# A gated state-space and linear-attention kernel: the convolution's kernel from two-factor tables by 32 channels, its parameters in polar form with n on the partitions, and FFT stages per 128 channels

## The chip, the cores and the metric

One core of one Trainium2 chip runs the kernel. The metric is the device time of one execution in microseconds (us), the median of the runs. Engines: PE is TensorE's matmul and PEld its weight load, DVE is VectorE, ACT is ScalarE, POOL is GpSimd, SP is SyncE, which here only issues DMAs.

## The reference

The input u has 2048 positions of 512 channels. Two branches are computed and mixed by a gate for each position:

```python
l = arange(L)                                        # L = 2048, D = 512, N = 128
P = exp(dt * A * l)                                  # complex, D x N x L
K = einsum("dn,dnl,dn->dl", Cc, P, dt * Bc).real
y = irfft(rfft(u padded to 2L) * rfft(K padded to 2L))[:L]
a = y + u * Dskip
pq, pk = q @ w_phi, k @ w_phi                        # 32 heads of 16
phi = concat(softmax(p), softmax(-p))
kv = sum_s phi_k v;  z = sum_s phi_k
b = ((phi_q @ kv) / (phi_q . z + 1e-6)) @ wo
g = sigmoid(sum(u * gate_w))
out = g * a + (1 - g) * b
```

## The kernel before

The program has four parts, one after the other. **Setup** loads u in two layouts (UD for the transform, xT for the attention), builds the transform's constants (TB, TI, TJ in `build_fft_consts`), turns A, B, C and dt into exponents and phases (`compute_params`) and writes these as pairs of bf16 rows through DRAM (pz) into four stationary tiles (statEL, statPL, statER, statPR). The spectrum of u, XU, is made here too (`u_path`). **Attention** (`part_b`) loads its weights, runs a loop over eight groups of 256 positions, multiplies all of Eq by the gate and denominator rows (aexp, L619 to L622), and then makes the output matmuls bps (L626, L628) into bS, which stays on chip.

**The convolution** goes over two halves of 256 channels (h). K of a channel is a product of a left factor (32 blocks of 64 positions) and a right factor (64 positions), summed over n on PE. Per 64 channels `exp_phase_q` makes E_L and E_R on ACT from argument matmuls. Per 32 channels `kgen_chunk` makes the phases: ACT computes k_y, k_anf, k_msinL, k_cosL, k_cosR, k_sinR; DVE multiplies them with E_L and E_R into k_Lre, k_mLim, k_Rre, k_Rim; PE makes 64 matmuls of 64 columns into kps (L234, L238); ACT casts to KD (L239), and `fft_stage_a` makes psA, evicted to XA. When all eight chunks are in XA, `k_slice_spectrum` runs over eight groups of two frequency rows: psB (L348), evicted to XK, two products t with XU on DVE (L380, L381), the inverse psz (L389), evicted to Z. Z is written to DRAM (Zd) and read back transposed (ZT) in two pieces, and `k_slice_out` makes psy, multiplies by the gate (ot) and writes the output. A scheduler orders each engine's instructions by its own estimates; buffers in the pools set what may run ahead.

Of the kernel before, what the change touches and what calls it, by code (L numbers as in the profile page):

```python
# [22 lines left out]

D = 512; N = 128; L = 2048


class KParams:
    pass


# [748 lines left out]
```

## Time and profile before

| | us |
|---|---|
| median of 3 runs (611.93 to 614.13) | 613.61 |
| profiled execution | 612.42 |
| its span | 609.9 |
| busy: ACT / PE / DVE / POOL | 309.9 / 304.6 / 285.4 / 51.6 |
| setup, until the attention's first matmul | 97.1 |
| attention | 140.0 |
| generator, spectrum, bounce and output, h = 0 | 115.4, 41.1, 28.2 |
| generator, spectrum, bounce and output, h = 1 | 113.8, 44.4, 29.9 |

No engine is busy for more than 51% of the span. The stages lie one after the other and have different limits, so the share of one engine over the span says little; each stage is to be read by itself, by what its last wait is for.

### The profile page before, as it was taken

The numbers are of one execution on the slowest core, as the hardware profiler recorded it, in microseconds if no ns is written. First come the engines' busy times: TensorE is split into PE (matmuls) and PEld (weight loads), VectorE is DVE, ScalarE is ACT, GpSimd is POOL, SyncE is SP. The second block draws the span as 40 slices with busy tenths as digits, with TensorE's granted clock in tenths as the row PEclk, the third lists the DMA queues.
The fourth block names the chain that finished last, engine by engine and source line by source line (L and its number), as shares of the span: only waits on it lengthen the run. The fifth ranks groups of instructions, "written<-read, shape, count | busy, mean of one in ns | idle before, by whom it ended". The sixth has DMA issues, their size and how long they took to land.

```text
span 609.9 us, 7578 instructions
## 1 busy us (share of the span) xinstructions
PE 304.6 (50%) x3168; PEld 150.0 (25%) x3168; DVE 285.4 (47%) x420; ACT 309.9 (51%) x384; POOL 51.6 (8%) x58
## 2 busy tenths in 40 slices
PE   0530346777858997252624346525252424356613
PEld 0430224433421353121212123301121212133300
DVE  6699953555567400626262645301626262635401
ACT  0541235799982125777768521106787768621202
POOL 7390570000000000000000000000000000000000
PEclk9975586899995799555557665655665768655555
DMA  9920280000000000000000003662000000001682
GB/s 256 234 43 1 70 205 6 0 1 0 2 2 0 1 0 1 0 1 1 0 2 0 2 1 97 103 82 66 0 1 1 0 2 0 2 1 72 68 138 69
DMA packets 44626, 23.31 MB, mean 38 GB/s; under 512 B 27952, under 2 KB 43312, under 8 KB 44080
## 3 DMA queue, kind: packets, MB, share of 16 engines
q1 hardware_dynamic: 21952, 12.59, 8.9%
q10 hardware_dynamic: 21488, 7.10, 7.2%
q0 software_dynamic: 1152, 3.15, 2.2%
q8 instruction: 24, 0.39, 0.3%
q14 instruction: 10, 0.08, 0.0%
HBM read 11.82 MB, written 9.96 MB: 36 GB/s over the span
## 4 chain that ended last, share of the span: by engine, by line
ACT 26%; PE 15%; DVE 6%; DMA 6%; issue 4%; ACTq 1%; SPq 0%
PE psz L389 5%; ACT E_R L189 4%; DMA ZT<-Zd 3%; PE psB L348 3%; PE psA L324 3%; ACT k_cosR L219 3%; ACT k_cosL L208 2%; ACT k_msinL L206 2%; ACT k_anf L204 2%; ACT k_sinR L220 2%; ACT E_L L181 2%; DVE t L380 2%; DVE XK L313 2%; ACT KD L239 2%; ACT L219 1%
## 5 line engine op out<-in xcount | busy, mean ns | idle before, releaser
L234 PE MATMUL kps<-k_Rre,k_Lre 128*32 128x64 bf16 x512 | 17.2, 241 | 102.9 <-DVE k_Lre L211 102.9
L190 DVE TENSOR_SCALAR nE_R<-E_R 128x2048 bf16<-128x2048 bf16 x8 | 5.6, 694 | 110.8 <-ACT E_R L189 110.8
L389 PE MATMUL psz<-t,TI 64*128 64x256 bf16 x256 | 30.6, 385 | 31.4 <-DVE t L380 31.4
L234 PEld LDWEIGHTS <-k_Lre 128*32 128x32 bf16 x512 | 13.7, 126 | 114.0 <-DVE k_Lre L211 114.0
L327 PE MATMUL psA<-W,UD 128*64 128x256 bf16 x128 | 13.9, 357 | 43.7 <-DMA UD<-in_A_u_dram 21.8
L626 PE MATMUL bps<-Mw,Eq 128*128 128x512 bf16 x128 | 31.8, 393 | 0.0
L189 ACT ACTIVATE E_R<-argps 128x1024 bf16<-128x1024 f32 x32 | 31.3, 1041 | 0.0
L630 ACT CAST bS<-bps 128x512 bf16<-128x512 f32 x16 | 9.4, 586 | 41.3 <-PE bps L628 41.3
L315 ACT CAST XK<-psB 128x1024 bf16<-128x1024 f32 x8 | 8.1, 1012 | 43.4 <-PE psB L348 43.4
L425 ACT ACTIVATE ot<-psy,gT 128x256 bf16<-128x256 f32 x16 | 6.7, 471 | 44.9 <-PE psy L416 35.4
L422 DVE TENSOR_TENSOR ot<-psy,gT 128x512 bf16<-128x512 f32 x8 | 5.5, 692 | 49.5 <-PE psy L416 38.6
L348 PEld LDWEIGHTS <-TB 64*64 64x64 bf16 x576 | 21.1, 146 | 30.4 <-issue 18.7
L186 PE MATMUL argps<-selR,statER 128*128 128x512 bf16 x64 | 25.4, 517 | 5.2 <-ACT E_R L189 2.9
L549 DVE TENSOR_TENSOR vr<-vp,vr 128x512 bf16<-128x512 f32 x32 | 19.9, 683 | 16.6 <-ACT vr L541 16.6
L239 ACT CAST KD<-kps 128x512 bf16<-128x512 f32 x16 | 9.4, 586 | 34.3 <-PE kps L238 34.3
L200 ACT ACTIVATE k_y<-argps 128x1024 f32<-128x1024 f32 x16 | 16.8, 1051 | 16.3 <-PE argps L197 16.3
L389 PEld LDWEIGHTS <-TI 64*128 64x128 bf16 x256 | 14.1, 121 | 41.5 <-DVE t L380 30.9
L537 DVE TENSOR_REDUCE Zk<-Ek 128x64 f32<-128x1024 bf16 x16 | 19.3, 1218 | 10.1 <-ACT Ek L536 9.5
L202 DVE SCALAR_TENSOR_TENSOR k_y<-k_y,argps 128x1024 f32<-128x1024 f32 x16 | 19.5, 1222 | 7.6 <-ACT k_y L200 7.6
L348 PE MATMUL psB<-XA,TB 64*64 64x128 bf16 (+1 forms) x384 | 21.1, 336 | 2.2 <-ACT XA L315 2.2
L324 PE MATMUL psA<-W,KD 128*128 128x256 bf16 x64 | 16.5, 414 | 11.0 <-ACT KD L239 11.0
L327 PEld LDWEIGHTS <-UD 128*64 128x64 bf16 x128 | 10.6, 202 | 45.3 <-issue 45.1
(222 smaller groups left out, 828.9 us busy)
## 6 DMA issues: line engine op xcount, KB each, us to landing
Zd<-Z SPq DMA_DIRECT2D x4, 1024.0 KB, 3.8
...
ZT<-Zd ACTq DMA_DIRECT2D x8, 256.0 KB, 8.0
ZT<-Zd SPq DMA_DIRECT2D x8, 256.0 KB, 7.6
out_dram<-ot SPq DMA_DIRECT2D x32, 32.0 KB, 1.6
out_dram<-ot ACTq DMA_DIRECT2D x32, 32.0 KB, 1.7
...
```

Source lines behind the costliest of these rows:

```text
L186: nc.tensor.matmul(ps[:, 8 * j:8 * j + 8, :], lhsT=kp.statER[:, G, :], rhs=kp.selR64[:, d0:d0 + 8, :], start=True, stop=True)
L189: nc.scalar.activation(out=E_R[:, dd:dd + 16, :], in_=ps[:], func=ACT.Exp)
L202: nc.vector.scalar_tensor_tensor(out=nf[:], in0=y[:], scalar=MAGIC, in1=ps[:], op0=ALU.subtract, op1=ALU.subtract)
L219: nc.scalar.activation(out=cosR[:], in_=ps2[:], func=ACT.Sin, scale=TWO_PI, bias=HALF_PI)
L234: nc.tensor.matmul(o, lhsT=Lre[:, dl, :], rhs=Rre[:, dl, :], start=True, stop=False, tile_position=(0, 32 * dj), skip_group_check=True)
L239: nc.scalar.copy(out=KD_dst, in_=kps[:].rearrange("p g e t -> p g (e t)"))
L324: nc.tensor.matmul(ps[:, i, :], lhsT=l[0], rhs=rhs, start=True, stop=True)
L327: nc.tensor.matmul(ps[64 * e:64 * e + 64, i, :], lhsT=l[e], rhs=rhs, start=True, stop=True, tile_position=(0, 64 * e))
L348: nc.tensor.matmul(o, lhsT=fc.TB[rows, r, op, :], rhs=rhs, start=(op == 0), stop=(op == 2), tile_position=(64 * e, 64 * rpar), skip_group_ ...
L389: nc.tensor.matmul(psz[:, rpar, sl, :], lhsT=fc.TI[rows, rh0 + sl, b0:b0 + 2, :].rearrange("p a b -> p (a b)"), rhs=rhs, start=(op == 0), ...
L549: nc.vector.tensor_tensor(out=vr[:, u, sg, :, 0:128].rearrange("p m (h e) -> p m h e", e=16), in0=vp[:].rearrange("p (m h e) -> p m h e", ...
L626: nc.tensor.matmul(ps[:], lhsT=Eq[:, i // 4, i % 4, 128 * j:128 * j + 128], rhs=Mw[:, i, :], start=(i == 0), stop=False, skip_group_check= ...
```

## The change

- **Tables in place of activations.** The left factor of K is no longer made by Exp and Sin for each channel block. Two tables with all 512 channels are made once, in setup: Ctab (4 factors for every 512 positions, with C, B and dt in it) and Dtab (8 factors for every 64 positions inside). `kgen_tables` multiplies them on DVE, complex, by broadcast: A has 4×8 = 32 columns per channel. Only the right factor comes from ACT: `kgen_exp` and `kgen_trig` for 128 channels at a time, in that order.
- **Parameters.** `polar_half` computes the tables from the raw parameters, which are loaded transposed (n on the partitions, channels along the row), in two halves of 256 channels. Only dt·A goes through pz into one tile, stat.
- **Weights' layout.** A has the channel as its innermost dimension, so kps's 32 weight columns are read 32 elements apart.
- **Four blocks of 128 channels** (Q) in place of two halves of 256. psB's matmuls have 128 and 64 columns where they had 256 and 128, psz's 128 where they had 256, with twice the number; eviction tiles keep their 1024 columns. KD, XA, XK and Z are all evicted on ACT, ot by DVE alone.
- **The bounce** is issued inside the loop over groups, when half of Z is there, and all of Zd, ZT and out stand in SP's queue. Rows of ZT and out are 256 bytes where they were 512. psy has a buffer of its own, so a block's output may run beside the next block's work.
- **Attention** alternates aexp and bps for each 512 positions, and bS goes through DRAM (bSd). Its weights are loaded early, in SP's queue; xp_d goes to ACT's queue and UD to POOL's, ahead of POOL's own work.

```diff
+    kp = Bag()
+    kp.stat = persist.tile([128, 16, 128], BF16, name="stat")
+    kp.C = persist.tile([128, 2, 4, 512], BF16, name="Ctab")
+    kp.D = persist.tile([128, 2, 8, 512], BF16, name="Dtab")
...
+def compute_polar(nc, tp, kp, raw):
+    for h in range(2):
+        polar_half(nc, kp, tp, {k: v[:, 256 * h:256 * h + 256] for k, v in raw.items()}, slice(256 * h, 256 * h + 256))
+    return kp
+def polar_half(nc, kp, tp, raw, ds):
+    nc.scalar.preload_act_table_set(LN_EXP)
...
+    EC = tp.tile([128, 4, W], BF16, name="EC", tag="e4", bufs=1)
+    nc.scalar.activation(out=EC[:], in_=big[:], func=ACT.Exp)
+    ED = tp.tile([128, 8, W], BF16, name="ED", tag="e8", bufs=1)
+    for b in range(8):
+        nc.scalar.activation(out=ED[:, b, :], in_=are[:], func=ACT.Exp, scale=64.0 * (b - 3.5))
...
+    sc = trig4(fill_c)
+    nc.vector.tensor_tensor(out=kp.C[:, 0, :, ds], in0=EC[:], in1=sc[:, 1], op=ALU.mult)
+    nc.vector.tensor_tensor(out=kp.C[:, 1, :, ds], in0=EC[:], in1=sc[:, 0], op=ALU.mult)
...
+def kgen_exp(nc, kp, selE, ps_pool, E, G0):
+    for gi in range(E.shape[1] // 32):
+        for b2 in range(2):
...
+            nc.scalar.activation(out=E[:, 32 * gi + 16 * b2:32 * gi + 16 * b2 + 16, :], in_=ps[:], func=ACT.Exp)
+def kgen_trig(nc, kp, selE, ps_pool, cs, G0):
+    for gi in range(cs.shape[2] // 32):
...
+        nc.scalar.activation(out=cs[:, 0, 32 * gi:32 * gi + 32, :], in_=ps[:], func=ACT.Sin, scale=TWO_PI, bias=HALF_PI)
+        nc.scalar.activation(out=cs[:, 1, 32 * gi:32 * gi + 32, :], in_=ps[:], func=ACT.Sin, scale=TWO_PI)
+def kgen_tables(nc, kp, wk, E, cs, dl, d0, n):
+    R = wk.tile([128, 2, n, 64], BF16, name="R", bufs=2)
+    Es = E[:, dl:dl + n, :]
+    c = cs[:, 0, dl:dl + n, :]; s = cs[:, 1, dl:dl + n, :]
+    ns = wk.tile([128, n, 32], BF16, name="ns", bufs=1)
+    nc.vector.tensor_scalar(out=ns[:], in0=s, scalar1=-1.0, scalar2=None, op0=ALU.mult)
+    nc.vector.tensor_tensor(out=R[:, 0, :, 32:64], in0=Es[:, :, 32:64], in1=c, op=ALU.mult)
+    nc.vector.tensor_tensor(out=R[:, 0, :, 0:32], in0=Es[:, :, 0:32], in1=c[:, :, ::-1], op=ALU.mult)
+    nc.vector.tensor_tensor(out=R[:, 1, :, 32:64], in0=Es[:, :, 32:64], in1=s, op=ALU.mult)
+    nc.vector.tensor_tensor(out=R[:, 1, :, 0:32], in0=Es[:, :, 0:32], in1=ns[:, :, ::-1], op=ALU.mult)
+    A = wk.tile([128, 2, 4, 8, n], BF16, name="A", bufs=2)
+    tmp = wk.tile([128, 4, 8, n], BF16, name="Atmp", bufs=1)
+    def Cb(i):
+        return kp.C[:, i, :, d0:d0 + n].unsqueeze(2).to_broadcast([128, 4, 8, n])
+    def Db(i):
+        return kp.D[:, i, :, d0:d0 + n].unsqueeze(1).to_broadcast([128, 4, 8, n])
+    for o, (i0, j0), (i1, j1), op in ((0, (0, 0), (1, 1), ALU.add), (1, (0, 1), (1, 0), ALU.subtract)):
+        nc.vector.tensor_tensor(out=A[:, o], in0=Cb(i0), in1=Db(j0), op=ALU.mult)
+        nc.vector.tensor_tensor(out=tmp[:], in0=Cb(i1), in1=Db(j1), op=ALU.mult)
+        nc.vector.tensor_tensor(out=A[:, o], in0=A[:, o], in1=tmp[:], op=op)
+    return A, R
+def kgen_chunk(nc, psK, A, R, dl, KD, ev):
+    kps = psK.tile([128, 4, 2, 64], F32, name="kps", tag="bk")
+    for e in range(2):
+        for g4 in range(4):
+            for ri in range(2):
+                for dj in range(4):
+                    d = dl + 16 * e + 4 * dj + g4
+                    nc.tensor.matmul(kps[32 * dj:32 * dj + 32, g4, e, :], lhsT=A[:, ri, :, :, d].rearrange("p a b -> p (a b)"),
+                                     rhs=R[:, ri, d, :], start=(ri == 0), stop=(ri == 1), tile_position=(0, 32 * dj), skip_group_check=True)
+    ev(KD, kps[:].rearrange("p g e t -> p g (e t)"))
...
+        step = 32 // ngr
+        if (2 * rh0 + 2 * ns) % step == 0:
+            r0 = 2 * rh0 + 2 * ns - step
+            rs = slice(r0, r0 + step)
+            nc.sync.dma_start(out=Zd[:, :, rs, :].rearrange("i t r d -> (i t) r d"), in_=Z[:, rs, :])
+            for th in range(2):
+                for ri in range(2):
+                    p0 = 64 * th + 32 * ri + r0
+                    eng = nc.sync if ri == 0 else nc.sync
+                    eng.dma_start(out=ZT[p0:p0 + step, :, :], in_=Zd[ri, 32 * th:32 * th + 32, rs, :].rearrange("t r d -> r t d"))
...
+    nj = min(512 // nd, 4)
+    for j0 in [x for jp in range(8 // nj) for x in (nj * jp, 8 + nj * jp)]:
+        th = j0 // 8
+        rows = slice(64 * th, 64 * th + 64)
+        ps = psY.tile([128, nj, nd], F32, name="psy", tag="py")
+        nc.tensor.matmul(ps[:], lhsT=ident[:], rhs=bsrc(j0, nj), start=True, stop=False, skip_group_check=True)
...
+        ot = opool.tile([128, nj, nd], BF16, name="ot")
+        nc.vector.tensor_tensor(out=ot[:], in0=ps[:], in1=gT[:, j0:j0 + nj].unsqueeze(2).to_broadcast([128, nj, nd]), op=ALU.mult)
+        ov = out2d[:, d0:d0 + nd].rearrange("(q j c) d -> c q j d", q=32, j=16, c=4)
+        for c in range(4):
+            nc.sync.dma_start(out=ov[c, :, j0:j0 + nj, :], in_=ot[32 * c:32 * c + 32, :, :])
...
-            nc.sync.dma_start(out=xp_d[512 * J:512 * J + 512, :].rearrange("(jc q) d -> jc q d", q=32), in_=xv[16 * J:16 * J + 16])
+            nc.scalar.dma_start(out=xp_d[512 * J:512 * J + 512, :].rearrange("(jc q) d -> jc q d", q=32), in_=xv[16 * J:16 * J + 16])
...
+        raw = {}
+        for k, src in (("Cre", A_C_re), ("Bre", A_B_re), ("Cim", A_C_im), ("Bim", A_B_im), ("Are", A_A_re), ("Aim", A_A_im)):
+            raw[k] = rawp.tile([128, 512], BF16, name=k)
+            nc.sync.dma_start_transpose(out=raw[k][:].unsqueeze(1), in_=src)
+        raw["ld"] = rawp.tile([128, 512], BF16, name="ld")
+        nc.gpsimd.dma_start(out=raw["ld"][:], in_=A_log_dt.partition_broadcast(128))
+        UD = rawp.tile([128, 64, 128], BF16, name="UD")
+        for dj in range(4):
+            nc.gpsimd.dma_start(out=UD[32 * dj:32 * dj + 32, :, :], in_=x2d[:, 128 * dj:128 * dj + 128].rearrange("(q t) d -> q t d", t=64))
...
+            def sink(j, ps):
+                bs = wp.tile([128, 512], BF16, name="bs", bufs=2)
+                nc.scalar.copy(out=bs[:], in_=ps[:])
+                nc.sync.dma_start(out=bSd[j], in_=bs[:])
+            attention(nc, tc, (wp, kpool, kwk, psB, psC), xT, wts, sink, gT, icol, ident, ck.close)
...
-        nd = 256
-        for h in range(2):
-            d0 = nd * h
+        nd = 128
+        n = 32
+        kev = Evict(nc, "a")
+        for Q in range(4):
+            d0 = 128 * Q
             XA = fpool.tile([128, 32, 2, nd // 2], BF16, name="XA")
...
+            E = epool.tile([128, 128, 64], BF16, name="E")
+            cs = epool.tile([128, 2, 128, 32], BF16, name="cs")
+            kgen_exp(nc, kp, selE, psP, E, 4 * Q)
+            kgen_trig(nc, kp, selE, psP, cs, 4 * Q)
+            for ch in range(4):
+                A, R = kgen_tables(nc, kp, wk, E, cs, 32 * ch, d0 + 32 * ch, n)
+                KD = wk.tile([128, 4, 128], BF16, name="KD", bufs=2)
+                kgen_chunk(nc, psK, A, R, 0, KD[:], kev)
+                fft_stage_a(nc, fc, psP, [[KD[:, i, :]] for i in range(4)],
+                            XA[:].rearrange("p r i (c d g) -> p (r i) c d g", d=4, g=4)[:, :, ch, :, :], kev)
             Z = fpool.tile([128, 32, nd], BF16, name="Z")
             ZT = fpool.tile([128, 32, nd], BF16, name="ZT")
-            Zd = dram.tile([2, 64, 32, nd], BF16, name=f"Zd{h}")
-            k_slice_spectrum(nc, fc, XA, nd, tpool, XU, d0, Z, Zd, ZT, psP, ev, evz)
-            k_slice_out(nc, fc, ident, ZT, nd, d0, bS, gT, out2d, opool, psP)
+            bS = fpool.tile([128, 16, nd], BF16, name="bS")
+            nc.sync.dma_start(out=bS[:], in_=bSd[:, :, d0:d0 + nd].rearrange("j p d -> p j d"))
+            Zd = dram.tile([2, 64, 32, nd], BF16, name=f"Zd{Q}")
+            k_spectrum_inverse(nc, fc, XA, nd, tpool, XU, d0, Z, Zd, ZT, psP, kev, kev, 2)
+            k_out(nc, fc, ident, ZT, nd, d0, lambda j0, nj: bS[:, j0:j0 + nj, :], gT, out2d, opool, psK)
```

ACT's order, the generator of 64 channels in the kernel before (E_L, E_R are exponentials, argps the arguments in PSUM, k_ tiles the phases of 32 channels):

```order
L181 ACTIVATE E_L<-argps 128x1024
L189 ACTIVATE E_R<-argps 128x1024 x2
L181 ACTIVATE E_L<-argps 128x1024
L189 ACTIVATE E_R<-argps 128x1024 x2
L200 ACTIVATE k_y<-argps 128x1024
L219 ACT_TABLE_LOAD
L219 ACTIVATE k_cosR<-argps 128x1024
L204 ACTIVATE k_anf<-k_y 128x1024
L206 ACTIVATE k_msinL<-k_y 128x1024
L208 ACTIVATE k_cosL<-k_anf 128x1024
L220 ACTIVATE k_sinR<-argps 128x1024
L239 CAST KD<-kps 128x512
```

In the changed kernel, the start of the generator for 128 channels; Z is the last eviction of the block before, E and cs are the tables of the right factor:

```order
L277 ACT_TABLE_LOAD
L277 ACTIVATE E<-args 128x1024
L70 CAST Z<-psz 128x2x4x128
L277 ACTIVATE E<-args 128x1024 x7
L286 ACT_TABLE_LOAD
L286 ACTIVATE cs<-args 128x1024
L287 ACTIVATE cs<-args 128x1024
```

All of the block's exponentials now stand together, and the phases of the left factor are gone.

DVE's order in the changed kernel, from the end of the first block's tables to its first product t12 (A_2439 belongs to that block's last 32 channels, finished just before; A_3049 and A_3137 to the first two chunks of the next block):

```order
L311 TENSOR_TENSOR Atmp_3050<-Ctab_288,Dtab_289 128x1024
L312 TENSOR_TENSOR A_3049<-A_3049,Atmp_3050 128x1024
L311 TENSOR_TENSOR Atmp_3050<-Ctab_288,Dtab_289 128x1024
L310 TENSOR_TENSOR A_3137<-Ctab_288,Dtab_289 128x1024
L312 TENSOR_TENSOR A_3049<-A_3049,Atmp_3050 128x1024
L310 TENSOR_TENSOR A_3137<-Ctab_288,Dtab_289 128x1024
L311 TENSOR_TENSOR Atmp_3138<-Ctab_288,Dtab_289 128x1024
L312 TENSOR_TENSOR A_3137<-A_3137,Atmp_3138 128x1024
L311 TENSOR_TENSOR Atmp_3138<-Ctab_288,Dtab_289 128x1024
L312 TENSOR_TENSOR A_3137<-A_3137,Atmp_3138 128x1024
L386 TENSOR_TENSOR t12_2576<-XU_60,XK_2574 128x1024
L387 TENSOR_TENSOR t34_2577<-XU_60,XK_2574 128x1024
```

The next block's left tables are made before the spectrum of this block is multiplied.

SP's order in the changed kernel, around the end of block 2 and block 3 (Zd_4272 is block 2's, Zd_5146 block 3's):

```order
L402 DMA Zd_4272<-Z 128x2048 x2
L407 DMA ZT<-Zd_4272 16x32x128 x8
L426 DMA out_dram<-ot 32x4x128 x4
L402 DMA Zd_5146<-Z 128x2048
L426 DMA out_dram<-ot 32x4x128 x12
L727 DMA bS<-bSd 128x16x128
L407 DMA ZT<-Zd_5146 16x32x128 x4
L402 DMA Zd_5146<-Z 128x2048
L407 DMA ZT<-Zd_5146 16x32x128 x4
L426 DMA out_dram<-ot 32x4x128 x16
```

The last 12 outputs of block 2 stand between the first half of block 3's Z and the reads of ZT.

## Rows read from the trace of the kernel before

**Rows 1.** Stage table: us, busy time and count of each engine, granted clock, DMA share.
```profile
0.00:97.10 97.10, 26.95 (x385) 19.36 (x386) 75.25 (x126) 27.13 (x28) 51.55 (x58) 0.76 0.57 128
97.10:237.10 140.00, 118.19 (x736) 55.77 (x737) 67.27 (x112) 87.30 (x141) 0.00 (x0) 0.89 0.00 1
237.10:352.50 115.40, 47.88 (x624) 21.04 (x624) 48.51 (x64) 84.64 (x91) 0.00 (x0) 0.60 0.00 1
352.50:393.60 41.10, 24.00 (x324) 13.95 (x325) 20.14 (x24) 9.10 (x9) 0.00 (x0) 0.62 0.30 52
393.60:421.80 28.20, 9.57 (x82) 2.89 (x82) 2.77 (x4) 5.43 (x10) 0.00 (x0) 0.50 0.56 108
421.80:535.60 113.80, 44.06 (x618) 19.94 (x618) 48.51 (x64) 83.83 (x90) 0.00 (x0) 0.66 0.01 2
535.60:580.00 44.40, 27.26 (x324) 14.95 (x325) 20.14 (x24) 9.11 (x9) 0.00 (x0) 0.50 0.28 48
580.00:609.90 29.90, 6.69 (x76) 2.05 (x75) 2.77 (x4) 3.36 (x8) 0.00 (x0) 0.50 0.54 106
```

**Rows 2.** Timeline of ACT, first generator; start, duration, line, operation.
```profile
238.75 1.93 ACT L189 ACTIVATE E_R<-argps 128x1024 bf16<-128x1024 f32 x2
...
244.37 1.28 ACT L219 ACT_TABLE_LOAD   x1
```

**Rows 3.** Timeline of all engines, end of one chunk's chain.
```profile
319.69 0.69 DVE L211 TENSOR_TENSOR k_Lre<-E_L,k_cosL 128x1024 bf16<-128x1024 bf16 x1 [0.25 <-ACT k_cosL L208]
320.43 0.11 PEld L234 LDWEIGHTS <-k_Lre 128*32 128x32 bf16 x4 [6.61 <-DVE k_Lre L211]
320.44 0.25 PE L234 MATMUL kps<-k_Rre,k_Lre 128*32 128x64 bf16 x4 [5.71 <-DVE k_Lre L211]
...
323.25 1.01 ACT L315 CAST XA<-psA 128x1024 bf16<-128x1024 f32 x1 [1.13 <-PE psA L324]
```

**Rows 4.** Timeline of ACT, second spectrum, first and last row.
```profile
535.63 1.01 ACT L315 CAST XA<-psA 128x1024 bf16<-128x1024 f32 x1 [1.13 <-PE psA L324]
...
578.96 1.01 ACT L315 CAST Z<-psz 128x1024 bf16<-128x1024 f32 x1 [3.15 <-PE psz L389]
```

**Rows 5.** Groups of PE, second spectrum: busy us, mean ns, idle before.
```profile
L389 PE MATMUL psz<-t,TI 64*128 64x256 bf16 x128 | 16.5, 410 | 15.7 <-DVE t L380 15.7
L348 PE MATMUL psB<-XA,TB 64*64 64x128 bf16 (+1 forms) x192 | 11.0, 346 | 1.1 <-ACT XA L315 1.1
```

**Rows 6.** Groups of DVE, first generator.
```profile
L202 DVE SCALAR_TENSOR_TENSOR k_y<-k_y,argps 128x1024 f32<-128x1024 f32 x8 | 9.8, 1222 | 3.8 <-ACT k_y L200 3.8
...
L225 DVE TENSOR_TENSOR k_Rre<-E_R,k_cosR 128x1024 bf16<-128x1024 bf16 x8 | 5.5, 684 | 0.0
```

**Rows 7.** Costliest groups of the page: weight loads from strided columns.
```profile
L327 PEld LDWEIGHTS <-UD 128*64 128x64 bf16 x128 | 10.6, 202 | 45.3 <-issue 45.1
```

**Rows 8.** DMA issues of the page: KB each, us to landing.
```profile
Zd<-Z SPq DMA_DIRECT2D x4, 1024.0 KB, 3.8
...
ZT<-Zd SPq DMA_DIRECT2D x8, 256.0 KB, 7.6
out_dram<-ot SPq DMA_DIRECT2D x32, 32.0 KB, 1.6
```

**Rows 9.** Timeline of DVE, the last output.
```profile
603.24 0.69 DVE L422 TENSOR_TENSOR ot<-psy,gT 128x512 bf16<-128x512 f32 x1 [1.66 <-DMA out_dram<-ot]
```

**Rows 10.** Timelines of ACT's queue, DVE and PE in setup.
```profile
0.80 13.45 ACTq L683 DMA_DIRECT2D UD<-in_A_u_dram  x4
...
32.05 2.19 DVE L290 TENSOR_SCALAR TI<-TI 128x2048 bf16<-128x2048 bf16 x1
...
97.10 1.12 PE L496 MATMUL wps<-Wphi,wkT 128*128 128x128 bf16 x9 [13.32 <-DMA Wphi<-in_B_w_phi_dram]
```

**Rows 11.** Timeline of PE, first output matmuls of the attention.
```profile
203.58 3.41 PE L626 MATMUL bps<-Mw,Eq 128*128 128x512 bf16 x8
...
207.05 1.89 PE L626 MATMUL bps<-Mw,Eq 128*128 128x512 bf16 x8
```

More of the change, by code (lines that the diff above doesn't have):

```diff
@@ new lines, in kgen_exp @@
+def kgen_exp(nc, kp, selE, ps_pool, E, G0):
+    for gi in range(E.shape[1] // 32):
+        for b2 in range(2):
+            ps = ps_pool.tile([128, 16, 64], F32, name="args", tag="pb")
+            for j in range(2):
+                d0 = 16 * b2 + 8 * j
+                nc.tensor.matmul(ps[:, 8 * j:8 * j + 8, :], lhsT=kp.stat[0:64, G0 + gi, :], rhs=selE[0:64, d0:d0 + 8, :],
+                                 start=True, stop=True, tile_position=(0, 0))
+            nc.scalar.activation(out=E[:, 32 * gi + 16 * b2:32 * gi + 16 * b2 + 16, :], in_=ps[:], func=ACT.Exp)
@@ L409, in k_slice_out, with k_out @@
+def k_out(nc, fc, ident, ZT, nd, d0, bsrc, gT, out2d, opool, psY):
+    nj = min(512 // nd, 4)
[4 more added lines that the diff above has]
+        nc.tensor.matmul(ps[:], lhsT=ident[:], rhs=bsrc(j0, nj), start=True, stop=False, skip_group_check=True)
         for jj in range(nj):
[L410 to L412 removed]
@@ L596, in part_b @@
-        for sg in range(2):
-            nc.vector.tensor_tensor(out=den[:, sg, :], in0=Sps[sg][:], in1=rZ[:, sg, :], op=ALU.mult)
-        nc.vector.tensor_tensor(out=den[:, 0, :], in0=den[:, 0, :], in1=den[:, 1, :], op=ALU.add)
-        nc.scalar.activation(out=den[:, 0, :], in_=den[:, 0, :], func=ACT.Ln, bias=eps[:])
-        nc.vector.tensor_tensor(out=lnZ[:], in0=lnZ[:], in1=den[:, 0:1, :].to_broadcast([128, 2, 512]), op=ALU.add)
-        nc.scalar.activation(out=apm[:], in_=lnZ[:], func=ACT.Exp, scale=-1.0)
@@ L615, in part_b @@
-        for b in range(4):
-            for m in range(4):
-                for sg in range(2):
-                    ps = bank("aexp")
-                    nc.tensor.matmul(ps[:], lhsT=Xsel[32 * b:32 * b + 32, m, :], rhs=apm[32 * b:32 * b + 32, sg, :], start=True, stop=True,
-                                     tile_position=(32 * b, 0))
-                    e = Eq[:, sg, m, 512 * b:512 * b + 512]
-                    nc.vector.tensor_tensor(out=e, in0=e, in1=ps[:], op=ALU.mult)
-        for j in range(16):
+                ps = bank("aexp")
@@ L624, in part_b @@
+                nc.tensor.matmul(ps[:], lhsT=Xsel[32 * b:32 * b + 32, m, :], rhs=apm[32 * b:32 * b + 32, sg, :], start=True, stop=True,
+                                 tile_position=(32 * b, 0))
+                e = Eq[:, sg, m, 512 * b:512 * b + 512]
+                nc.vector.tensor_tensor(out=e, in0=e, in1=ps[:], op=ALU.mult)
+        for j in range(4 * b, 4 * b + 4):
             ps = bank("bps")
```

811 lines of the change are left out of this document (341 added, 470 removed).

## The prediction

> **What bounds the kernel now.** I read the stage table first [rows 1]. The profiled execution spans 609.9 us and took 612.42, so 2.5 us lie outside the span; it stands 1.2 us under the median of 613.61. Six of the eight stages do the convolution: twice a generator (115.4 and 113.8), a spectrum (41.1 and 44.4) and a bounce through DRAM with the output (28.2 and 29.9), 372.8 us together. In the generator ACT is busy 84.64 of 115.4 us, DVE 48.51, PE 47.88. In the bounce no engine works: PE 9.57 of 28.2, DMA 0.56. The generator's limit is a chain. ACT makes tables of 128x1024, two E_R in 1.93 us at 238.75, so 0.92 or so apiece, with 1.28 for a table load [rows 2]; per 128 channels it makes 36 (4 E_L, 8 E_R, and per 32 channels k_y, anf, msinL, cosL, cosR, sinR), with 4 table loads. Then ACT waits while the last table goes DVE → PE → ACT → PE → ACT [rows 3]: k_Lre runs from 319.69 to 320.38, kps starts at 320.44, XA at 323.25 and ends at 324.26, so 3.9 us pass from the table's end to XA's.
>
> The spectrum follows a generator and runs from XA's end at 536.64 to the last Z's end at 579.97, 43.3 us for 256 channels, at a granted clock of 0.50 (the 1.2 GHz level) [rows 1, 4]. PE waits there for t: psB x192 and psz x128 are 11.0 and 16.5 us busy of 43.3 [rows 5], and the rest is PE → eviction → t → PE → eviction with little overlap.
>
> **The generator.** ACT now makes per 128 channels 8 Exp (L277) and 8 Sin (L286/L287), with 2 table loads, in place of 36 and 4; ACT's rows in the second order fence show it. That is 20×0.92 + 2×1.28 [rows 2] = 21 us less of ACT per 128 channels. What comes in its place is DVE work: per 32 channels 6 two-input operations on the broadcast tables C and D (A, Atmp), 4 for R and a negation. For R and A the row is k_Rre L225, bf16 128x1024 at 684 ns [rows 6], which starts every 0.61 when back to back. L225 reads one input with step −1 at this price; no row reads bf16 inputs with step 0. So A's price lies between 0.61 and the 1.22 of the f32 operation of the same size [rows 6]; I take 0.61, since A's operands and result are bf16 as L225's are, and keep 1.22 for the range.
>
> By the Trainium skill, "VectorE: DVE Perf Modes", section "What auto-detection actually checks", a two-input operation takes its doubled mode where every tensor is 16-bit with step ±1; a step of 0 in an outer dimension is left open by that sentence. Row L225 agrees for step −1. If the mode were lost, the sum would be the one with 1.22 below; if not, mine.
>
> Each block of 128 channels is then a chain, and DVE's order (third fence) says where it can hide. The tables A of the next block's first two chunks stand ahead of the first t of the spectrum, so they cost nothing as long as DVE waits there for XA and XK; if that cover fails, 12×0.61 = 7 us come back per block. From the last Z: ACT has one E ahead of that Z, then 7×0.92 + 1.28 + 1.05 = 8.8 us to the first cosine. DVE then has 28 operations (16 R, 12 A of the last two chunks) × 0.61 and 4 negations of some 0.4 (half of 0.69): 18.7. The last chunk's kps → XA is 3.9 as now [rows 3]; its 64 matmuls take 0.9 us now, from 320.44 on, with four loads at a time. Its weights are now read with a stride of 32 elements; the nearest row is UD's, strided too, 202 ns a load [rows 7]. Four at a time, 64 such loads would take 3.2 us: the far bound is +2.3 per block. I take zero, since the loads overlap. The spectrum for 128 channels is half of 43.3: 21.7, since the number of evictions, t and columns halves. That is 53.1. Four psy/ot of the block before, set between XK and Z, add 1.5 (4 ot of 0.69 less what falls into waits), and I add 1.4 for more and narrower matmuls: **56 per block**, 224 for four, against 314.7 for the two generators and spectra [rows 1].
>
> The narrower matmuls are the main doubt. For the same 1024 columns per group psB now takes 48 matmuls instead of 24, and psz 32 instead of 16: over the kernel 1280 where 640 were. A matmul of 64 columns can follow the one before at 14 ns (64 kps in 0.9 us), so columns set the pace, not counts: about zero. The other bound keeps all of today's spectrum time in PE's count: 27.5 us over 320 matmuls [rows 5] is 86 ns for each, so 640 more are +55.
>
> **The bounce.** Block Q's Zd, ZT, psy and out now lie beside block Q+1's generator; for three of four blocks nothing waits for them. Before, 28.2 us in the middle were bare; I put that at 0. The cover is 35 us of generator against 3.8 (Zd) + 7.6 (ZT) and the outputs [rows 8]. At the end stays one bounce. Per block it is half as large, but SP's order (fourth fence) puts 12 outputs of block 2 between the two halves of Zd and all of ZT, and PE has eight psy behind the last psz. An ot waits for its buffer until earlier outputs have landed, as now at 603.24 (1.66 us, [rows 9]), so I count 2 us for each group of four outputs, of which landing is 1.6. That makes 4×2 for block 2's outputs, Zd and ZT 3.8 + 7.6, four psy/ot 4×2.1, and from the last ot's start to the end 6.7 as now (603.24 to 609.9): 34.5, some 35 instead of 29.9, **+5**.
>
> The Trainium skill, "DMA: Bandwidth & Descriptors", section "Specifications", speaks against this part: under 512 bytes a transfer leaves line rate, with a read-modify-write, and ZT and out now go in rows of 256 bytes. No row here tells 256 from 512 for ZT; if ZT took as long as today for half the bytes, 7.6 us, the sum above has it so already.
>
> **Setup.** Before, the first wps starts at 97.10, after 13.32 us of waiting for Wphi's loads [rows 10]; these now stand early in SP's queue, so the wait goes. But POOL now issues UD ahead of its own iotas: ACT needed 13.45 us for these four issues [rows 10], and DVE's constants (TI ends at 34.24 now) start some 10 us later: 45. Then the tables C and D: two halves of 256 columns, each a chain that goes back and forth between DVE (some 45 operations, 16 us by the rates of [rows 6] scaled to their columns) and ACT (12 us and 7 table loads of 1.28, 9 us), 37 alone, about 65 for both with one's ACT beside the other's DVE. With the last XU that puts wps at 111: **+14**, bounds −12 (all of the constants' delay hidden and the halves overlapped better) and +12.
>
> **Attention.** From 97.1 to 237.1 it takes 140.0 [rows 1]. Its loop is unchanged, two table loads per round included. The products Eq and the output matmuls alternate per 512 rows now, so each of the four output runs starts behind a stretch at half clock: the first eight bps matmuls of a run take 3.41 against 1.89 [rows 11], 3 times 1.5 more, with aexp's first latency and shorter evictions: **+6** (0 to +16). The first front, which has nothing beside it, adds 1.6.
>
> **Sum.** 609.9 + 14 + 6 + 1.6 − (314.7 − 224) − 28.2 + 5 = 517.6, with 2.5 outside **520 us**.
>
> **Rivals.** (a) A at the slow rate: 12 operations of the last two chunks per block × 0.61 is +7 to +8 per block, 552. For: no row with step 0; against: everything is bf16. (b) The spectrum is bound by the count of matmuls: +55, 575. For: PE is the longest link there; against: kps's 14 ns. (c) The bounce is not hidden, since SP's one queue holds Zd, ZT and out in an order in which each waits for the one before, and psy, in the middle of PE's order, holds back psz: up to 10 per block in three blocks, 550. (d) Slower than before: every added matmul costs its full latency, because four row and column tiles no longer overlap when each has half the columns. At psB's mean of 336 ns [rows 5] 640 more are +215, 735; it decides from (613.6 − 520)/640 = 146 ns each. The kps chain is against it. (e) The setup's chain overlaps fully and the spectrum reaches full clock (4.2 for 5.2 us in each of 16 groups): −12 − 16, 492.
>
> **How the numbers follow.** The forecast's case (500 to 545) 0.66, (a) 0.10, (b) 0.08, (c) 0.07, (e) 0.04, (d) 0.03, 0.02 for no change, should several of (a) to (c) meet. The range of 494 to 560 leaves out (b), (d) and the lower edge of (e). Change by less than 0.5%, 3 us, is about what a measurement of this kernel can't tell: faster 0.94, same 0.01, slower 0.05.
>
> **What would show it.** In the new profile: ACT busy some 32 of 56 us in a block; A (L310 to L312) near 0.69 mean; psB and psz with about unchanged total busy time for twice the count; no stretch of 28 us without engines in the middle; the first wps near 111; the last Z some 35 us before the end. The prediction is wrong if A has 1.2 in its row, if the time from XA to the last Z in a block is well over 22, or if setup lasts beyond 123.

## The result and the profile after

The changed kernel takes 541.18 us, median of 4 runs (540.47 to 541.62), against 613.87 (611.93 to 615.76) for the kernel before in the same session: ratio 0.8815, 95% interval 0.8786 to 0.8844. The forecast was 520 in a range of 494 to 560, so the gain is 73 us where 94 were expected. The profiled execution took 540.47, its span 538.7.

The stage table of the changed kernel, to be laid beside [rows 1], has the same columns. The first three rows are the setup up to the attention's first matmul wps at 141.16, the next two the attention (its loop; aexp and bps), then four blocks and the end:

```profile
0.00:34.80 34.80, 0.00 (x0) 0.18 (x1) 3.70 (x20) 0.01 (x1) 8.34 (x17) 1.00 1.08 177
34.80:88.00 53.20, 20.86 (x192) 15.35 (x192) 34.59 (x55) 27.20 (x38) 11.38 (x6) 1.00 0.37 85
88.00:141.30 53.30, 17.17 (x194) 9.13 (x194) 38.90 (x79) 39.47 (x50) 1.80 (x5) 1.00 0.00 1
141.30:229.50 88.20, 65.67 (x507) 34.71 (x513) 50.82 (x81) 77.03 (x122) 0.00 (x0) 0.96 0.00 1
229.50:281.00 51.50, 47.89 (x220) 20.61 (x222) 20.08 (x33) 9.35 (x16) 0.00 (x0) 0.86 0.12 38
281.00:336.90 55.90, 33.41 (x622) 20.17 (x622) 38.89 (x65) 32.57 (x37) 0.00 (x0) 0.53 0.17 32
336.90:394.10 57.20, 36.34 (x684) 21.77 (x683) 33.71 (x56) 31.66 (x36) 0.00 (x0) 0.50 0.15 29
394.10:449.60 55.50, 34.10 (x635) 20.66 (x634) 31.82 (x53) 31.64 (x35) 0.00 (x0) 0.50 0.34 51
449.60:502.50 52.90, 34.18 (x679) 20.85 (x678) 25.45 (x43) 29.23 (x33) 0.00 (x0) 0.53 0.38 59
502.50:538.70 36.20, 8.06 (x119) 3.14 (x118) 5.10 (x8) 0.02 (x1) 0.00 (x0) 0.50 0.65 102
```

Against the forecast's sum:

| us | forecast | measured | off |
|---|---|---|---|
| setup | 111.1 | 141.3 | +30.2 |
| attention | 146.0 | 139.7 | −6.3 |
| four blocks, with the first front | 225.6 | 221.5 | −4.1 |
| the end | 34.9 | 36.2 | +1.3 |
| span | 517.6 | 538.7 | +21.1 |

The convolution came out near its sum; the miss lies in the setup. For 34.8 us hardly an engine works, and then PE, DVE and ACT are busy for 38, 73 and 67 of another 106.

**The setup.** Timelines of the changed kernel, several engines; start, duration, engine, line, and in brackets the idle time before it and what ended it:

```profile
0.80 33.97 ACTq L639 DMA_DIRECT2D xp_d<-in_A_u_dram  x4
...
2.19 4.20 POOL L648 DMA_DIRECT2D UD<-in_A_u_dram  x4
...
34.80 1.28 ACT L182 ACT_TABLE_LOAD   x1 [34.80 <-DMA gw<-in_gate_w_dram]
...
37.82 1.29 DVE L84 TENSOR_SCALAR tg_v<-colB,if_p 128x2048 int32<-128x2048 f32 x1 [27.99 <-ACT w L87]
...
52.98 1.45 DVE L115 TENSOR_SCALAR TI<-TI 128x2048 bf16<-128x2048 bf16 x1
```

POOL needed 4.20 us for the four UD issues, not 13.45 as ACT in [rows 10]; its delay, which the forecast counted, is not there. ACT stands instead: the four xp_d issues hold its queue from 0.80 to 34.77, so it makes its first table entry at 37.38, DVE waits 27.99 us for it, and TI is done at 54.4, where it was done at 34.2 before [rows 10]. The row of 33.97 us is mostly waiting. All operations on xp_d (ns, shortest, median and longest; first and last start), and the profile's chain around the fourth issue (start, duration):

```profile
L639 ACTq DMA_DIRECT2D xp_d<-in_A_u_dram x4: 570/584/696, 0.8 to 34.2; - x4
```

```profile
29.92 4.25 DMA gw<-in_gate_w_dram
...
34.20 0.57 ACTq L639
```

An issue takes 0.57 to 0.70 us; the rest lies between them. The second starts at 25.08, when SP's transposed load Are has landed (issued at 6.16, landing 18.9 us later), the third at 27.18, with the landing of wkT (19.09, 8.1 later), the fourth behind the landing of gw. In the trace's records these three issues wait for the completion semaphores of Are, wkT and gw. So ACT waits for SP's loads, though it needs none of the three tiles yet. No run changes the semaphores alone.

The second loss is in the matmuls of u's spectrum. Groups of PE from 34 to 142 us in the changed kernel (busy, mean ns, idle before them and what ended it):

```profile
L338 PE MATMUL psA<-W,UD 128*64 128x256 bf16 x128 | 18.4, 422 | 56.6 <-DVE W L100 39.9 <-DVE XAu L68 9.6 <-ACT XAu L70 7.1
L359 PE MATMUL psB<-XAu,TB 64*64 64x256 bf16 (+1 forms) x192 | 17.1, 484 | 42.8 <-DVE XU L68 19.2 <-ACT XU L70 16.9 <-ACT XAu L70 6.7
```

psB waits 19.2 and 16.9 us for evictions XU. The full diff has a change that I hadn't shown or costed: `psA` and `psB` lost `bufs=3`. In the convolution they take the three buffers of their pool, but `u_path` runs in a pool of one (`ps0`), so each group of matmuls waits for the eviction of the one before, and each eviction stands in line between the polar operations on ACT and DVE.

**A block.** Groups from 281 to 502.5 us, to be laid beside [rows 5, 6]:

```profile
L395 PE MATMUL psz<-t,TI 64*128 64x128 bf16 x512 | 35.4, 305 | 30.7 <-DVE t L386 30.5 <-DVE t L387 0.2
...
L312 DVE TENSOR_TENSOR A<-A,Atmp 128x1024 bf16<-128x1024 bf16 x32 | 21.9, 685 | 0.4
L310 DVE TENSOR_TENSOR A<-Ctab,Dtab 128x1024 bf16<-128x1024 bf16 x32 | 21.5, 681 | 7.9 <-PE bps L604 7.9
L324 PE MATMUL kps<-R,A 128*32 128x64 bf16 x1024 | 21.2, 246 | 21.5 <-DVE A L312 18.5 <-DVE R L300 2.9
L359 PE MATMUL psB<-XA,TB 64*64 64x64 bf16 (+1 forms) x768 | 20.1, 265 | 4.4 <-ACT XA L70 4.4
```

A by broadcast has 681 and 685 ns for 128x1024, the rate of k_Rre (684). psB and psz are shorter each, 265 and 305 ns where the second spectrum had 346 and 410. All of psB is 20.1 us for 768 matmuls; the same group over both halves of the kernel before has 21.1 us for 384.

ACT in the last block, to be laid beside [rows 2, 4]:

```profile
449.50 6.53 ACT L277 ACTIVATE E<-args 128x1024 bf16<-128x1024 f32 x7
456.05 1.28 ACT L286 ACT_TABLE_LOAD   x1
...
479.90 1.01 ACT L70 CAST XA<-psA 128x1024 bf16<-128x1024 f32 x1 [1.12 <-PE psA L335]
...
501.51 1.01 ACT L70 CAST Z<-psz 128x1024 bf16<-128x1024 f32 x1 [3.09 <-PE psz L395]
```

From XA's end (480.91) to the last Z's end (502.52) there are 21.6 us; the forecast had 21.7. This is the shortest of the four blocks. All of them, read the same way (us):

| block | 1 | 2 | 3 | 4 | forecast |
|---|---|---|---|---|---|
| from the block before's last Z to XA | | 31.7 | 31.7 | 31.3 | 31.4 |
| from XA to the last Z | 22.5 | 25.5 | 23.8 | 21.6 | 21.7 |

The forecast had 2.9 a block more, outside of these two rows, for psy, ot and narrower matmuls: on the mean of the four blocks the second row exceeds 21.7 by 1.7.

### The profile page after: what moved, and what is told of

Its sections match the earlier page's. It is cut to its first block, busy times and chain, and to the rows that moved or that the text cites. A ratio compares the mean times of both kernels' runs of the same rounds, so it can differ in the third digit from the quotient of the medians.

```text
span 538.7 us, 9011 instructions
## 1 busy us (share of the span) xinstructions
PE 297.7 (55%) x3845; PEld 166.6 (31%) x3856; DVE 283.1 (53%) x489; ACT 278.2 (52%) x359; POOL 21.5 (4%) x28
## 4 chain that ended last, share of the span: by engine, by line
ACT 30%; DVE 30%; PE 25%; SPq 8%; issue 4%; DMA 3%; ACTq 0%; DVEq 0%
PE psz L395 6%; PE bps L602 6%; ACT E L277 5%; SPq L643 3%; DVE A L312 3%; DVE A L310 3%; DVE Atmp L311 3%; ACT XK L70 2%; PE pk L511 2%; SPq L652 2%; DVE t L386 2%; PE psB L359 2%; PE psA L338 2%; DVE R L299 2%; ACT Z L70 2%
## 5 line engine op out<-in xcount | busy, mean ns | idle before, releaser
L395 PE MATMUL psz<-t,TI 64*128 64x128 bf16 x512 | 35.4, 305 | 30.7 <-DVE t L386 30.5
L70 ACT CAST Z<-psz 128x1024 bf16<-128x1024 f32 x16 | 16.2, 1012 | 47.6 <-PE psz L395 47.6
L359 PE MATMUL psB<-XAu,TB 64*64 64x256 bf16 (+1 forms) x192 | 17.1, 484 | 42.8 <-DVE XU L68 19.2
L602 PE MATMUL bps<-Mw,Eq 128*128 128x512 bf16 x124 | 34.9, 429 | 0.9 <-DVE Eq L598 0.7
L598 DVE TENSOR_TENSOR Eq<-Eq,aexp 128x512 bf16<-128x512 bf16 x32 | 19.5, 679 | 26.7 <-PE aexp L595 26.7
L324 PE MATMUL kps<-R,A 128*32 128x64 bf16 x1024 | 21.2, 246 | 21.5 <-DVE A L312 18.5
L277 ACT ACTIVATE E<-args 128x1024 bf16<-128x1024 f32 x32 | 30.1, 1052 | 2.9 <-PE args L275 2.9
L275 PE MATMUL args<-selE,stat 64*128 64x512 bf16 x64 | 27.2, 587 | 1.6 <-ACT E L277 0.9
L324 PEld LDWEIGHTS <-A 128*32 128x32 bf16 x1024 | 17.7, 151 | 31.6 <-DVE A L312 22.2
L310 DVE TENSOR_TENSOR A<-Ctab,Dtab 128x1024 bf16<-128x1024 bf16 x32 | 21.5, 681 | 7.9 <-PE bps L604 7.9
L70 ACT CAST XA<-psA 128x1024 bf16<-128x1024 f32 x16 | 16.2, 1012 | 18.0 <-PE psA L335 18.0
## 6 DMA issues: line engine op xcount, KB each, us to landing
UD<-in_A_u_dram POOLq DMA_DIRECT2D x4, 512.0 KB, 17.1
```

The source lines that it names most:

```text
L70: self.nc.scalar.copy(out=out, in_=in_)
L275: nc.tensor.matmul(ps[:, 8 * j:8 * j + 8, :], lhsT=kp.stat[0:64, G0 + gi, :], rhs=selE[0:64, d0:d0 + 8, :], start=True, stop=True, tile_po ...
L277: nc.scalar.activation(out=E[:, 32 * gi + 16 * b2:32 * gi + 16 * b2 + 16, :], in_=ps[:], func=ACT.Exp)
L310: nc.vector.tensor_tensor(out=A[:, o], in0=Cb(i0), in1=Db(j0), op=ALU.mult)
L324: nc.tensor.matmul(kps[32 * dj:32 * dj + 32, g4, e, :], lhsT=A[:, ri, :, :, d].rearrange("p a b -> p (a b)"), rhs=R[:, ri, d, :], start=(r ...
L359: nc.tensor.matmul(o, lhsT=fc.TB[rows, r, op, :], rhs=rhs, start=(op == 0), stop=(op == 2), tile_position=(64 * e, 64 * rpar), skip_group_ ...
```

## The experiments

Theory 1: the setup is longer by two separate delays, ACT held in its queue and one PSUM buffer; each can be taken away alone. Theory 2: the polar chain itself is what costs. The first batch takes these apart.

**Three PSUM buffers again.**

```diff
-    ps = ps_pool.tile([128, 4, 256], F32, name="psA", tag="pb")
+    ps = ps_pool.tile([128, 4, 256], F32, name="psA", tag="pb", bufs=3)
-    ps = ps_pool.tile([128, 2, ns, 2, ncol], F32, name="psB", tag="pb")
+    ps = ps_pool.tile([128, 2, ns, 2, ncol], F32, name="psB", tag="pb", bufs=3)
```

> The changed kernel, with three PSUM buffers again for psA and psB (as before the change), where its u path has one. Theory 1: the setup is long because ACT sits 34 us behind xp_d's issues and because, with one buffer, each XAu and XU eviction waits for its turn between the polar operations of ACT and DVE. Then the 16 psA tiles take some 20 us instead of 42, XU no longer follows the polar chain, and the first wps moves from 141.2 to about 121, the time from 541 to about 521. Theory 2: the polar chain with its 14 table loads sets the setup whatever the buffers: the last polar operation stays where it is, the first wps moves by less than 6 us and the attention waits for nothing else: 535 to 541.

528.28 us in one run, 12.9 less than the change and between the two theories' times. The same groups of PE, from 34 to 142 us:

```profile
L338 PE MATMUL psA<-W,UD 128*64 128x256 bf16 x128 | 13.9, 374 | 44.8 <-DVE W L100 41.2 <-DVE XAu L68 2.3 <-ACT XAu L70 1.3
L359 PE MATMUL psB<-XAu,TB 64*64 64x256 bf16 (+1 forms) x192 | 12.0, 400 | 13.0 <-DVE XU L68 11.0 <-DVE XAu L68 2.0
```

The wait for XU falls from 36.1 us to 11.0, and wps starts at 88 instead of 141. Only 12.9 of these 53 us reach the end. ACT's polar operations run to 130.8, and the casts of wps stand behind them; PE's next work waits 32 us for the last of these:

```profile
131.39 1.85 PE L479 MATMUL gps<-gw,xT 128*128 128x1 bf16 x64 [32.08 <-ACT Wqp L471]
```

**xp_d in SP's queue.**

```diff
-            nc.scalar.dma_start(out=xp_d[...], in_=xv[16 * J:16 * J + 16])
+            nc.sync.dma_start(out=xp_d[...], in_=xv[16 * J:16 * J + 16])
```

> The changed kernel, with xp_d's four copies back at the head of SP's queue. Theory 1: ACT's first table load comes at about 10 instead of 34.8; psA's start moves from 39.9 to about 24.5, when UD has landed, and all of the setup with it: 15 us, about 526. If the transposes on SP come later for it and the raw parameters or xT become the last wait, less: 530 to 541. Theory 2 says the same shift as theory 1, as the polar chain starts behind psA.

530.78 in one run, 10.4 less. Timeline of this kernel:

```profile
0.80 1.28 ACT L182 ACT_TABLE_LOAD   x1 [0.80 <-PEq L769]
0.80 5.11 SPq L639 DMA_DIRECT2D xp_d<-in_A_u_dram  x4
...
21.14 1.12 PE L338 MATMUL psA<-W,UD 128*64 128x256 bf16 x8 [21.14 <-DMA UD<-in_A_u_dram]
```

The same four issues end after 5.11 us where they stand ahead of SP's other loads, ACT starts at 0.80, and psA at 21.14 (39.85 in the change, 21.84 before) waits for data alone. Theory 1 had 15 us, though: psA starts 18.7 us earlier, but its sixteen tiles take 51 us to pass instead of 41, and wps starts at 132.1, 9 earlier.

**Both.** 

> Both edits, three buffers and xp_d on SP. Theory 1: the two delays lie one behind the other, so they add: first wps near 105, total about 505. Theory 2: only the shift of the queue shows, 526.

517.4 (516.6 to 518.15), ratio to the kernel before 0.844 (0.8407 to 0.8474): 23.8 less, the sum of the two (12.9 and 10.4). My size for it (505) was too large, and one window shows what comes next:

```profile
78.10:121.00 42.90, 4.34 (x36) 3.42 (x33) 27.02 (x60) 33.94 (x46) 1.42 (x5) 0.50 0.00 0
```

The last XU is evicted by 82, and PE is busy 4.34 of 42.9 us. The polar chain runs from 59.8 to 123 on ACT and DVE, and the casts of the attention's first weights wait in line behind it.

**No polar chain.** C and D are filled with zeros by POOL, and `compute_polar` is left out.

```diff
-            compute_polar(nc, pool(cc, "ptmp"), kp, raw)
+            nc.gpsimd.memset(kp.C[:], 0.0)
+            nc.gpsimd.memset(kp.D[:], 0.0)
```

> The changed kernel without the polar computation: the tables C and D are filled with zeros, everything after them runs as before on them. Theory 1: the u path goes on at the pace of one buffer, 2.33 us a tile, so XU takes some 37 instead of 53 us and psA as now: first wps near 122, total about 522. Theory 2: the polar chain was the length of the setup: first wps below 105, total below 505.

520.12 in one run, 21.1 less, with wps at 118.23, near theory 1's 522 and 122. The chain of some 65 us is worth 21 as long as the two delays stand: theory 2 as the only cause falls.

The second batch asks where the remaining time can go.

**Tables of two chunks left out.** In each block chunks 0 and 1 (first kernel) or 2 and 3 (second) read a tile of zeros as A.

```diff
+    if A0 is not None:
+        return A0, R
...
-                A, R = kgen_tables(nc, kp, wk, E, cs, 32 * ch, d0 + 32 * ch, n)
+                A, R = kgen_tables(nc, kp, wk, E, cs, 32 * ch, d0 + 32 * ch, n, A0 if ch in (0, 1) else None)
```

> The changed kernel, but the left tables A of the first two chunks of each block are not computed: these chunks read a tile of zeros (48 DVE operations of 0.68 us fewer in all, and wrong K for half of the channels). The prediction's claim is that these operations lie beside the last chunk's chain and the wait for XK and cost nothing: 541 (within 4, some 1 us a block for the t that they hold back). If instead DVE is what a block waits for all along, 48 times 0.61 are saved: 512.

> The same for the last two chunks of each block: 48 DVE operations fewer, those that the prediction puts on the path. By it the four blocks are shorter by 12 times 0.61 each, 29 us, until ACT's cosines and sines (ended 8 us behind the first R) set the pace: 515 to 522. If A is hidden here too (PE or ACT being the limit of a block): 535 to 541.

518.58 and 523.59, one run each. The second lies 1.6 above its expectation. The first missed: leaving out the tables that the forecast called hidden saves as much as leaving out the others. The four blocks take 199.2 and 200.2 us in the two kernels, instead of 221.5, some 5.5 a block. (Half of the 5.0 between the two times lies in the setup, which neither edit touches: in the four kernels with the change's setup wps starts between 139.6 and 143.5, so a single run can be off by two us for that alone.) I read it from DVE's order: two buffers for A are filled ahead of the spectrum with whatever two sets there are. What a block pays for is then what goes beyond two sets, not chunks 2 and 3 as such. The kernels with four buffers, below, test this.

**Outputs from POOL's queue**, on top of both repairs.

```diff
-            nc.sync.dma_start(out=ov[c, :, j0:j0 + nj, :], in_=ot[32 * c:32 * c + 32, :, :])
+            nc.gpsimd.dma_start(out=ov[c, :, j0:j0 + nj, :], in_=ot[32 * c:32 * c + 32, :, :])
```

> Three PSUM buffers and xp_d on SP as in the run before with both edits (517.4), and the outputs issued from POOL's queue, which is empty by then, not from SP's. Theory: in the last bounce the second half of Zd is issued 12 us after Z is there, because SP's queue holds block 2's outputs ahead of it, each of which waits for its ot; without them Zd and ZT go at once, the end is some 10 us shorter: 507. Rival: psy and ot (one PSUM buffer, two ot buffers) set the pace of the end whatever the queue, or POOL's slower issues (0.75 each) take it back: 514 to 518.

519.25 in one run, against 517.4: no gain. Windows of the kernel with both repairs, then of this one (blocks, end):

```profile
261.00:479.00 218.00, 132.18 (x2615) 79.65 (x2614) 129.88 (x217) 124.88 (x135) 0.00 (x0) 0.55 0.26 43
479.00:516.20 37.20, 8.07 (x119) 3.15 (x118) 5.07 (x8) 0.00 (x0) 0.00 (x0) 0.50 0.63 100
```

```profile
261.00:487.20 226.20, 134.67 (x2631) 80.93 (x2630) 130.54 (x217) 125.16 (x135) 19.58 (x36) 0.54 0.24 44
487.20:517.50 30.30, 6.87 (x102) 2.70 (x101) 4.37 (x7) 0.00 (x0) 15.15 (x28) 0.50 0.65 100
```

The end is 6.9 us shorter, so outputs in SP's queue do cost there, but the blocks are 8.2 longer. One place is `psy<-bS` on PE at 374.66, which waits 2.65 us for the load of bS; ACT's next E waits behind PE. The third block, where this is, loses 5.0 of the 8.2, 3.3 of them ahead of its first cosine. Where the rest went stays open.

**The polar chain inside the attention**, on top of both repairs: it is issued ahead of the aexp loop, so that it may lie beside the attention's own work. Raw parameters stay on chip until then.

```diff
-            compute_polar(nc, pool(cc, "ptmp"), kp, raw)
...
+    polar()
     for b in range(4):
         for m in range(4):
```

> Both edits, and the polar computation moved from setup to the attention, between its row sums and its products with aexp (the raw parameters stay in SBUF until then; nothing is left out). In the changed kernel ACT is busy 9.35 and DVE 20.08 of the 51.5 us of that stage. Theory 1 (in the setup the polar chain and the u path stand in each other's way, and with both edits the polar chain is what is left): the setup ends near 75, the attention's loop takes 88 as before, the last stage grows to some 65 at most since the chain of 53 us runs beside it: total 485 to 495. Rival: aexp and bps wait for the polar operations on ACT and DVE, one behind the other, and the stage grows by the whole chain: 512 or more.

489.93 (488.48 to 490.93), ratio 0.8007 (0.7976 to 0.8039). Windows of the attention's loop and of aexp and bps:

```profile
63.20:150.00 86.80, 67.14 (x509) 34.12 (x513) 53.38 (x94) 72.67 (x119) 0.63 (x1) 0.95 0.01 2
150.00:229.90 79.90, 54.09 (x224) 21.76 (x228) 52.99 (x109) 55.31 (x82) 0.00 (x0) 0.74 0.08 25
```

wps starts at 63.2. The second stage grows from 51.5 to 79.9 us, so the chain is still not free; of some 63 us, 28 show. The time lies inside the expectation by two misses that cancel: the setup ends 12 us earlier than the 75 expected, and the stage is 15 longer than 65. The granted clock there is 0.74 instead of 0.86.

**Four buffers for A**, a test of the reading of the two kernels without tables: in the change alone, and with all the rest.

```diff
-    A = wk.tile([128, 2, 4, 8, n], BF16, name="A", bufs=2)
+    A = wk.tile([128, 2, 4, 8, n], BF16, name="A", bufs=4)
```

> The changed kernel with four buffers for A where it had two; nothing else is touched. Theory (cover): a block pays only for the tables that do not fit into the buffers ahead of it, since two of four chunks stood in the waits of the spectrum whichever half was left out; with four buffers all 24 operations of the next block can stand there. Then the R operations alone stand between the sines and the last kps, and a block loses the 5.3 to 5.6 us that leaving out a half gave: three blocks by 5.5, about 525 us, with the waits of DVE for XK filled by L310 to L312. Rival (DVE is the limit of the block as a whole): moving operations inside it changes nothing, 541. Second rival: the tables now stand ahead of the products t in DVE's order and hold them, so that the spectrum grows by as much as the generator loses, 538 to 545, with Z later after XA than 21.6 us.

> The version with three PSUM buffers, xp_d in SP's queue and the polar chain beside the attention, now with four buffers for A as well. If the blocks gain by the buffers as in the changed kernel, and the attention, which also has to take the first block's two further sets of tables (7 us of DVE), has DVE time left for them, 489.9 less some 14 to 17: 473 to 478. If the rival holds (DVE is the limit of the block, or the tables hold back t), 486 to 493. Theory: 475.

528.86 in one run, 12.3 less than the change. Its blocks, and DVE in the second one:

```profile
280.00:336.40 56.40, 32.90 (x620) 19.95 (x619) 45.25 (x75) 32.52 (x36) 0.00 (x0) 0.52 0.17 32
336.40:389.00 52.60, 35.10 (x668) 20.80 (x666) 33.11 (x55) 32.02 (x36) 0.00 (x0) 0.50 0.14 27
389.00:440.00 51.00, 32.73 (x637) 20.35 (x637) 31.14 (x52) 32.18 (x36) 0.00 (x0) 0.60 0.38 58
440.00:491.00 51.00, 34.26 (x695) 20.56 (x693) 19.51 (x33) 28.48 (x31) 0.00 (x0) 0.50 0.41 63
```

```profile
365.84 0.69 DVE L387 TENSOR_TENSOR t<-XU,XK 128x1024 bf16<-128x1024 bf16 x1
366.44 0.69 DVE L311 TENSOR_TENSOR Atmp<-Ctab,Dtab 128x1024 bf16<-128x1024 bf16 x1
...
371.40 0.68 DVE L386 TENSOR_TENSOR t<-XU,XK 128x1024 bf16<-128x1024 bf16 x1
```

Of the 12.3 us, 10.2 lie between the last bps and the last Z; 1.6 are the setup's, which differs from run to run (wps at 139.6). Blocks 2 to 4 take 154.6 us instead of 165.6. By the ends of their last Z, and in the same two parts as above:

| block | 1 | 2 | 3 | 4 |
|---|---|---|---|---|
| whole, change | | 57.2 | 55.5 | 52.9 |
| whole, four buffers | | 52.2 | 50.5 | 51.6 |
| last Z to XA, four buffers | | 26.4 | 27.0 | 29.5 |
| XA to last Z, four buffers | 24.0 | 25.8 | 23.5 | 22.1 |

Blocks 2 and 3 gain 5.0 each, near the theory's 5.5. The first gains none: its tables wait for the attention's last bps in either kernel (L310 starts at 280.40 in the change, after 7.94 us of waiting for it), and ACT's first E follows at once, so there is no wait of DVE's ahead of it to fill. The last gains 1.4 only; three ot of the block before (456.28 to 462.28) now lie among its R, but no run tests whether that is the cause. The second rival isn't borne out: tables do stand between two products t (366.44 to 371.40), but from XA to the last Z blocks 2 to 4 take 71.4 us in all, where the change takes 70.9. Only the first block is longer there, by 1.5. That DVE limits the block as a whole falls.

With everything together 476.74 (473.44 to 477.33), ratio 0.7753 (0.7719 to 0.7786), as expected and the shortest of the study: 64 us less than the change, with nothing left out.

## Why the prediction was right, and where it was off

**What failed: the setup, +14 where it is +44, outside of its own bounds.** The step is "POOL now issues UD ahead of its own iotas ... DVE's constants ... start some 10 us later". A duration was taken from ACT's queue (13.45) and put on POOL's; there the issues take 4.20 us, and with xp_d in SP's queue TI ends at 34.7, 0.5 later than before (36.7 with both repairs). The work that did move onto a path, xp_d on ACT ahead of the tables' first entry, got no price at all, though the description of the change and the diff named it; it is worth 10.4 us. And the lost `bufs=3`, worth 12.9, was read over in a long diff. Together the two are 23.8 of the 30 missing. The remaining 6 fit the polar chain's start, though no run shows this alone: it was put right behind the constants at 45, but with both repairs it starts at 59.8, behind the evictions of XAu. Its length, 65 forecast, is 63 with three buffers and 71 in the change (68.3 to 138.9). By the prediction's own sign (a setup beyond 123) this part is wrong. That the time still lies in the range is partly luck: the range is 66 us wide, and the attention and the blocks came in 10 us under.

**Attention, +6, was about zero.** The trace of before splits its 140.0 us into 88.4 and 51.6; after, it is 88.2 and 51.5. Slow first bps are there in three of four rounds, but in two of them not behind a stretch at half clock, and with a counterpart that I left out. PE in the changed kernel, second round:

```profile
242.59 1.53 PE L595 MATMUL aexp<-apm,Xsel 32*128 32x512 bf16 x5
...
246.15 4.00 PE L602 MATMUL bps<-Mw,Eq 128*128 128x512 bf16 x11 [0.23 <-DVE Eq L598]
```

The first eleven bps take 4.57, 4.00, 2.53 and 4.22 us in the four rounds, where eleven at 1.89 for eight would be 2.6: +4.9, against 1.5 of the kind before [rows 11]. But eight aexp now take 3.6 us (242.59 to 246.15), where 32 took 18.08 in a row, 4.5 for eight: 0.9 less in each of four rounds. The gain and the loss are of one size. The granted clock is the last figure but two of a window; here the 32 aexp of the kernel before, then the second round's aexp and part of its first bps:

```profile
185.50:203.58 18.08, 17.63 (x32) 3.39 (x32) 17.47 (x30) 0.90 (x2) 0.00 (x0) 0.50 0.00 0
```

```profile
242.59:246.15 3.56, 2.65 (x11) 0.76 (x10) 3.13 (x6) 0.59 (x1) 0.00 (x0) 1.00 0.12 41
247.50:249.00 1.50, 1.50 (x5) 0.49 (x4) 0.39 (x1) 0.00 (x0) 0.00 (x0) 0.50 0.04 11
```

In rounds 2 to 4 the aexp stand behind a run of bps and go at the upper level (2.4 GHz); in rounds 2 and 4 the clock falls only in the bps after them. In the third it stays at 1.00 through the first eleven bps, 2.53 us.

**Blocks, right.** 55.4 us each with the first front, 56.4 forecast. Right were A at the rate of [rows 6], PE paced by columns rather than by matmuls (twice the count at psB's 20.1 us for 21.1 and psz's 35.4 for 30.6, with XA to Z between 21.6 and 25.5 for half of 43.3 and the 2.9 added), and weights with a stride: kps's loads are 151 ns, 126 to 128 before, and their matmuls wait for DVE's tables, not for loads; from the last table's end (476.9) to XA's end there are 4.0 us, 3.9 forecast. By the Trainium skill, "VectorE: DVE Perf Modes", section "What auto-detection actually checks", the doubled mode wants 16-bit tensors with step ±1; the trace's 681 ns for A shows that a step of 0 in an outer dimension doesn't lose it. Rivals (a), (b) and (d) fall with these rows ((d)'s 336 ns is psB's mean over both spectra; [rows 5] has 346), and (e) with the setup's length and the blocks' granted clock of 0.50 to 0.53. One argument of the step was too simple: "the tables of the next block's first two chunks cost nothing" holds for two sets, whichever they are, as far as there are buffers: leaving out chunks 0 and 1 saved as much as leaving out 2 and 3, and four buffers took 5.0 us off blocks 2 and 3.

**The bounce, right.** No stretch is without engines in the middle. At the end 36.2 us for 34.9, in the order foreseen. DMA issues of the page (KB each, median us to landing), to be laid beside [rows 8]:

```profile
Zd<-Z SPq DMA_DIRECT2D x8, 512.0 KB, 4.8
ZT<-Zd SPq DMA_DIRECT2D x32, 128.0 KB, 5.1
```

SP's queue at the end:

```profile
504.62 0.38 SPq L402 DMA_DIRECT2D Zd<-Z  x1
...
505.10 5.99 SPq L426 DMA_DIRECT2D out_dram<-ot  x12
...
514.67 0.43 SPq L402 DMA_DIRECT2D Zd<-Z  x1
...
526.25 0.62 PE L420 MATMUL psy<-ZT,TJ 64*32 64x128 bf16 x16 [9.47 <-DMA ZT<-Zd]
```

The second half of Zd is issued 12 us after the last Z, behind twelve outputs and the first ZT, as forecast. Rival (c) had up to 10 us a block for this queue; the blocks show none of that size, though moving the outputs away cost as much as it gave. The Trainium skill, "DMA: Bandwidth & Descriptors", section "Specifications", has transfers under 512 bytes below line rate: ZT takes 5.1 us for half of the bytes that took 7.6, more than half. No run separates the row's length from the size.
